# Banded attention with a gated MLP on one core: first values and w_in loaded as whole rows, all loads on SyncE in a planned order

## The chip, the cores and the metric

One core of a Trainium2 chip runs the whole kernel in one launch. The metric is the device time of one execution in microseconds, taken as the median of several runs. Next to it there is one execution recorded by the hardware profiler, from which all rows below come.

## The reference

For 8 batches of 576 positions and 8 heads of 64 columns, attention looks back over a band (32 positions in the first four heads; 128 positions, every fourth one, in the other four). Its output goes through a gated MLP whose gate mixes positions:

```python
scores = where(mask, q @ k.T / sqrt(64), -1e9);  attn = softmax(scores);  x = attn @ v      # x: 8 x 576 x 512
h = maximum(x @ w_in, 0)                          # w_in 512 x 1024
u, v = h[..., :512], h[..., 512:]
v_n = (v - mean(v)) / sqrt(var(v) + 1e-6)
v_s = einsum('ts,bsd->btd', w_spatial, v_n) + b_spatial[None, :, None]      # w_spatial 576 x 576
out = (u * v_s) @ w_out                           # w_out 512 x 512
```

`w_in` and `w_out` come as 64-bit floats, so each is converted on the chip.

## The kernel before, in words

Every large matrix product is made three times, from a rounded ("high") and a remainder ("low") copy of both factors (`PASSES`), so each weight has to be turned into a high and a low tile first. The tiles are `wi` (w_in), `wo` (w_out) and `wt`, `wa`, `wb` (w_spatial), each ending in h or l.

The work of a batch is cut into strands, Python generators that ask for one engine at a time:
- `unit`: scores, maximum, exponential, sum, scaling and transposition of a third of a group of two head pairs. There are six in a batch (group 0 and group 1, three thirds each). PE does the scores at L558, the maximum's subtraction at L623 and the transposition at L573.
- `weighted` (L708): the product with the values of one group, 152 small matmuls. `evacuated` takes the result from PSUM into `xt`.
- `v_tile` (L772): the second half of `x @ w_in`, in five tiles of positions; `gate` (L839, L849 to L851): the first half, and the mixing of positions; `project` (L874): the product with `w_out`, and the store of `ob` to `out`.
- `weight` turns one 128 x 512 part of `w_in` or `w_out` (64-bit) into high and low: ACT L420, L450 and L455, DVE L424 and L426, and two more operations (an add at L433 or L436, a subtraction at L369 or L372) that go to POOL where the table `BY_POOL` has an 'a' or an 's' and else to DVE. `spatial` does the like with `w_spatial`, with the table `EXTRA` for the engine.
- `heads_in`, `values_in`, `weight_in` and `spatial_in` load keys and queries (`kq`), values (`val`), 64-bit weights and `w_spatial` (`stage`).

The class `Timeline` (a planner that runs when the program is built) decides the order on every engine: it always takes the strand with the least value of predicted start plus 0.196 times its rank. `SHIFTS` moves single ranks, `LOADS` sets the order of the first loads. What the planner fixes is the order alone; on the chip each instruction waits on semaphores.

Three things about the loads matter here. `values_in` makes four DMAs for each pair of heads, each of 32 rows with 9 strips of 256 bytes (72 KB), into one of three `val` buffers. `weight_in` needs one of four `stage` buffers, which are idle parts of the later `gated` tiles; a half of `w_in` is two DMAs of 64 rows by 4 KB, one issued by SyncE (L385) and one by ScalarE's queue (L396). A buffer is given back when its conversion is done. The stores of `ob` (L881 to L886) are issued by SyncE where the planner happens to reach them: they take no time of its DMA resource. [...]

`warm` (L896) puts matmuls of zeros on PE at the start, up to a planned time of 20 us, whenever nothing else is ready by the plan.

Of the kernel before, what the change touches and what calls it, by code (L numbers as in the profile page):

```python
# [13 lines left out]
F32 = mybir.dt.float32  # L14
# [46 lines left out]
LOADS = [0, 1, 2, 3, 5, 10, 4, 6, 9, 16, 8, 12, 14, 17, 22, 15, 19, 20, 25, 18, 7, 21, 24, 11, 26, 23, 13]  # L61
BY_POOL = {
    (0, 0): '', (0, 1): 'as', (0, 2): 'a', (0, 3): 'as', (1, 0): '', (1, 1): 'as',
    (1, 2): 'as', (1, 3): 's', (2, 0): 's', (2, 1): 'as', (2, 2): 'a', (2, 3): 'a',
}
EXTRA = {
    ('soft', 0, 0, 0): 0, ('soft', 0, 0, 1): 0, ('soft', 0, 0, 2): 0, ('soft', 0, 1, 0): 0, ('soft', 0, 1, 1): 0, ('soft', 0, 1, 2): 0,
# [944 lines left out]
```

## Time and profile before

| what | value |
|---|---|
| median of 3 runs | 577.76 us (577.19 to 841.0) |
| the profiled execution's own time | 578.02 us |
| its span | 576.2 us |
| PE busy in the span | 547.3 us (95%), 7826 matmuls |
| DVE, ACT, POOL busy | 291.6, 222.1, 130.0 us |

The span runs from the first to the last recorded event; the other 1.82 us of the profiled execution lie around it. PE's busy time is the sum of its matmuls' durations, so 28.9 us of the span have no matmul at all. [...]

### The profile page before, as it was taken

Reading aid. Unit: us, or ns where it says so; the run is one execution under the profiler, and the core shown is the slowest. Engines: PE = TensorE matmul, PEld = TensorE weight load, DVE = VectorE, ACT = ScalarE, POOL = GpSimd, SP = SyncE. Lnnn points to the kernel's source line nnn. Section 1 sums busy time; section 2 is a strip of 40 time slices with the busy share of each in tenths; the row PEclk is TensorE's granted clock in tenths of the full one; section 3 lists DMA queues with packets and bytes.
Section 4 is the critical chain, followed back from the end, with each engine's and each line's share of the span. In section 5 each row is a group of like instructions: output and inputs, shape, how many; then the busy total and the mean of one; then the engine's idle time right before and its main releaser. Section 6 shows DMA issues by size and latency. Waiting matters only on the chain.

```text
span 576.2 us, 17989 instructions
## 1 busy us (share of the span) xinstructions
PE 547.3 (95%) x7826; PEld 500.2 (87%) x7826; DVE 291.6 (51%) x735; ACT 222.1 (39%) x557; POOL 130.0 (23%) x161
## 2 busy tenths in 40 slices
PE   7878989999999999999999999996998999999997
PEld 5656879979998789999989879995897899999997
DVE  5766995456466266344365445591645352314220
ACT  2556855334334334242344432251423152224222
POOL 2536761233033023002133101241302100000000
PEclk9969999999999899999999999998999999999999
DMA  8897714232135310012342530124102101001002
GB/s 223 189 232 191 262 36 122 61 131 97 42 80 177 89 38 1 1 63 76 118 128 51 160 76 1 41 69 126 55 22 53 23 3 52 7 25 42 22 11 83
DMA packets 62882, 47.20 MB, mean 82 GB/s; under 512 B 43730, under 2 KB 52946, under 8 KB 62804
## 3 DMA queue, kind: packets, MB, share of 16 engines
q1 hardware_dynamic: 62164, 43.97, 27.3%
q10 hardware_dynamic: 640, 2.10, 1.4%
q8 instruction: 61, 1.00, 0.7%
q14 instruction: 17, 0.14, 0.1%
HBM read 36.61 MB, written 9.44 MB: 80 GB/s over the span
## 4 chain that ended last, share of the span: by engine, by line
PE 81%; DMA 8%; DVE 6%; issue 2%; SPq 2%; ACT 1%; ACTq 0%; DVEq 0%
PE bank L874 17%; PE bank L849 17%; PE bank L839 17%; PE bank L772 14%; PE bank L708 5%; PE bank L558 5%; DMA stage<-in_w_in_dram 3%; PE bank L573 3%; DMA val<-in_vw_dram 2%; PE bank L851 1%; PE bank L850 1%; DMA kq<-in_qT_dram 1%; SPq L546 1%; DVE mid L426 1%; PE bank L623 1%
## 5 line engine op out<-in xcount | busy, mean ns | idle before, releaser
L874 PE MATMUL bank<-gh,woh 128*128 128x288 f32 x256 | 78.6, 307 | 0.1
L854 DVE TENSOR_TENSOR ur<-ur,bank 128x288 f32<-128x288 f32 x64 | 28.9, 451 | 98.0 <-PE bank L851 98.0
L839 PE MATMUL bank<-xth,wih 128*128 128x288 f32 x256 | 77.8, 304 | 0.4 <-DVE vs L369 0.4
L849 PE MATMUL bank<-wth,vnh 128*128 128x288 f32 x256 | 77.0, 301 | 0.0
L874 PE MATMUL bank<-gl,woh 128*128 128x288 f32 x256 | 76.0, 297 | 0.1
L874 PE MATMUL bank<-gh,wol 128*128 128x288 f32 x256 | 76.0, 297 | 0.0
L849 PE MATMUL bank<-wth,vnl 128*128 128x288 f32 x256 | 75.5, 295 | 0.0
L849 PE MATMUL bank<-wtl,vnh 128*128 128x288 f32 x256 | 75.4, 295 | 0.0
L839 PE MATMUL bank<-xth,wil 128*128 128x288 f32 x256 | 75.4, 294 | 0.0
L839 PE MATMUL bank<-xtl,wih 128*128 128x288 f32 x256 | 75.4, 294 | 0.0
L790 POOL TENSOR_TENSOR stats<-stats,halfneg 128x1 f32<-128x1 f32 (+1 forms) x37 | 23.3, 631 | 183.7 <-DVE stats L788 183.6
L772 PE MATMUL bank<-wih,xth 128*128 128x512 f32 (+1 forms) x148 | 61.2, 414 | 0.2 <-DVE vnl L369 0.2
L643 POOL TENSOR_TENSOR pg<-pg,nm 128x384 f32<-128x384 f32 x36 | 32.3, 898 | 120.8 <-DVE nm L641 111.5
L772 PE MATMUL bank<-wil,xth 128*128 128x512 f32 (+1 forms) x148 | 59.0, 399 | 0.0
L772 PE MATMUL bank<-wih,xtl 128*128 128x512 f32 (+1 forms) x148 | 58.8, 397 | 0.0
L652 POOL TENSOR_TENSOR pg<-pg,rv 128x384 f32<-128x384 f32 x48 | 42.2, 880 | 73.1 <-DVE rv L650 57.7
L878 ACT COPY ob<-bank 128x288 f32<-128x288 f32 x64 | 25.7, 401 | 75.7 <-PE bank L874 53.2
L860 ACT CAST gh<-ur 128x288 fp32r<-128x288 f32 x64 | 27.3, 437 | 63.5 <-DVE ur L854 54.1
L874 PEld LDWEIGHTS bank<-gh,woh 128*128 128x128 f32 x256 | 48.7, 190 | 1.8 <-ACT gh L860 0.4
L839 PEld LDWEIGHTS bank<-xth,wih 128*128 128x128 f32 x256 | 48.0, 188 | 1.7 <-DVE vs L369 0.5
L874 PEld LDWEIGHTS bank<-gl,woh 128*128 128x128 f32 x256 | 48.8, 191 | 0.6 <-DVE gl L369 0.3
L849 PEld LDWEIGHTS bank<-wth,vnh 128*128 128x128 f32 x256 | 48.2, 188 | 0.7
(105 smaller groups left out, 1099.5 us busy)
## 6 DMA issues: line engine op xcount, KB each, us to landing
val<-in_vw_dram SPq DMA_DIRECT2D x128, 72.0 KB, 2.8
kq<-in_kT_dram SPq DMA_DIRECT2D x30, 304.0 KB, 3.7
kq<-in_qT_dram SPq DMA_DIRECT2D x30, 288.0 KB, 4.0
out_dram<-ob SPq DMA_DIRECT2D x48, 144.0 KB, 1.8
stage<-in_w_in_dram ACTq DMA_DIRECT2D x8, 256.0 KB, 6.1
stage<-in_w_in_dram SPq DMA_DIRECT2D x8, 256.0 KB, 5.5
stage<-in_w_out_dram SPq DMA_DIRECT2D x4, 512.0 KB, 4.5
out_dram<-ob SPq DMA_DIRECT2D x16, 112.0 KB, 1.8
```

Of the source, the lines that this page charges most:

```text
L558: nc.tensor.matmul(s[j][q * QB : q * QB + QB], kq[r, WIN + S :].rearrange("p (u n i t) -> p u t n i", n=2, i=QB, t=US)[:, u, g // 2 % US, ...
L643: nc.gpsimd.tensor_add(flat, flat, nm.unsqueeze(2).broadcast_to([P, 2 * US, KW]))
L652: nc.gpsimd.tensor_mul(flat, flat, rv.unsqueeze(2).broadcast_to([P, 2 * US, KW]))
L708: nc.tensor.matmul(acc[h, j][1][1][i * D : i * D + D, at : at + len(blocks) * QB], values[b, hp][1][r, kb // 2 * D : kb // 2 * D + D], x, ...
L772: nc.tensor.matmul(pm, xt[a][:, c, at : at + m], wi[w][:, c, NF:], start=c == 0 and n == 0, stop=c == NC - 1 and n == 2)
L790: nc.gpsimd.tensor_tensor(rs[:m], rs[:m], halfneg[:m], op=ALU.pow)
L839: nc.tensor.matmul(pu, wi[w][:, c, fs], xt[a][:, c, xs], start=n == 0, stop=n == 3 * NC - 1)
L849: nc.tensor.matmul(pv, vn[c][a][:, fs], wts[w][:, c, ws], start=n == 0, stop=False)
L854: nc.vector.tensor_mul(ur, ur, pv)
L860: nc.scalar.copy(gated[0][:, f, ts], ur)
L874: nc.tensor.matmul(po, wo[w][:, f, ds], gated[a][:, f, ts], start=n == 0, stop=n == 3 * NC - 1)
L878: nc.scalar.copy(ob[1], po)
```

## The change

- The values of batch 0 are loaded as whole rows of 4,608 bytes that hold both halves (j = 0 and 1), 32 rows to a DMA, four DMAs for each pair. They land in the memory of the later `wt` tiles (`wide`), not in `val` buffers. The matmuls read the half that they need.
- `w_in` is loaded in four chunks of 128 whole rows (8 KB a row, both halves of `w_in` at once; two DMAs of 64 rows each). Each chunk has its own place: the two `gated` tiles and the two tiles of the later `wo`. No load of `w_in` waits for a buffer. The `stage` buffers of `w_spatial` and `w_out` come into being when the first two chunks have been converted.
- The conversion of `w_spatial` waits until both `weighted` of batch 0 are done, and that of `w_out` until chunks 2 and 3 are converted, since they write into that memory.
- ScalarE issues no DMA any more. SyncE issues all.
- The planner has a new model of the DMAs, and the stores of `ob` now take a place in SyncE's plan.
- A small activation at the head of ScalarE's program, before the first real one.
- New numbers in `SHIFTS`, `LOADS`, `BY_POOL` (21 instead of 15 of 24 operations on POOL), `EXTRA` (all five low parts of `w_spatial` on POOL, before four) and in some planner costs. With the new order `warm` issues 35 matmuls instead of 6.

```diff
-LOADS = [0, 1, 2, 3, 5, 10, 4, 6, 9, 16, 8, 12, 14, 17, 22, 15, 19, 20, 25, 18, 7, 21, 24, 11, 26, 23, 13]
+LOADS = [0, 1, 17, 4, 2, 21, 18, 14, 3, 16, 8, 15, 5, 13, 20, 6, 9, 19, 22, 7, 11, 12, 10]
 BY_POOL = {
-    (0, 0): '', (0, 1): 'as', (0, 2): 'a', (0, 3): 'as', (1, 0): '', (1, 1): 'as',
-    (1, 2): 'as', (1, 3): 's', (2, 0): 's', (2, 1): 'as', (2, 2): 'a', (2, 3): 'a',
+    (0, 0): 'as', (0, 1): 'as', (0, 2): 'a', (0, 3): 'as', (1, 0): 'a', (1, 1): 'as',
+    (1, 2): 'as', (1, 3): 'as', (2, 0): 'as', (2, 1): 's', (2, 2): 'as', (2, 3): 'as',
 }
...
-        self.free = {"DMA": 1.68, "PE": 1.0}
+        self.free, self.moved = {"DMA": 0.72, "PE": 1.0}, 0.0
...
-        late = 1.15 if engine == "DMA" else 0.0
+        late = 0.1 if engine == "DMA" else 0.0
...
             if s.engine == "DMA":
-                self.queue.append((start, start + cost))
+                first, cost = max(start + 0.9, self.moved), s.request[2]
+                self.moved = max(first + s.request[1], start + cost + 0.7)
+                self.queue.append((first, self.moved))
+                landed = self.moved + 0.9
...
-            stage=[t[:, n * BIG : (n + 1) * BIG] for t in stage for n in range(2)],
+            stage=[],
...
+    stage += [const.tile([P, NC * DM], F32, name=f"wos{n}", tag=f"wo{n}") for n in "hl"]
+    wide = [const.tile([P, 4 * (TAIL + S)], F32, name=f"wide{n}", tag=f"wt{n}") for n in "hl"]
...
-    def weight_in(key, src):
+    def pieces_in(c):
 
+        yield DMA, 3.0, 1.2
+        tile = stage[c]
...
+        for n in range(2):
+            row = (c // 2 * 4 + c % 2 + 2 * n) * D
+            nc.sync.dma_start(
+                place[n * D : n * D + D].bitcast(dtype), w_in[row : row + D].rearrange("r h k -> r (h k)")
+            )
...
+            c = key[2]
+            tl.tally(("read", c), 2, [("chunk", c)], [("stage", stage[c][:, n * BIG : n * BIG + BIG]) for n in range(2)] if c < 2 else [])
...
-        yield [("in", sc)]
+        yield [("in", "sp", sc)] + [("weighted", 0, G) for G in range(NG)] * (sc < 4)
...
     def values_in(b, hp):
 
+        if b == 0:
+            yield DMA, 1.45, 0.6
+            dst = wide[hp // 2][:, hp % 2 * BIG : hp % 2 * BIG + BIG]
+            for n in range(2):
+                k = WIN + (1 - n) * QB
+                for j in range(2):
+                    nc.sync.dma_start(dst[j * D + n * QB : j * D + n * QB + QB], vw[b, hp, k : k + QB])
...
-                                values[b, hp][1][r, kb // 2 * D : kb // 2 * D + D],
+                                values[b, hp][j][r, kb // 2],
...
         nc.scalar.copy(ob[1], po)
         tl.give(*held)
+        yield DMA, 0.42, 0.85 if b % 2 and h == 0 else 0.4
...
+    nc.scalar.activation(turnstile, halfneg, AF.Exp)
     tl.add(0.5, warm())
```

Three places show what the planner made of it. The first is SyncE's own order where the first loads stand. `kq` are keys and queries, `stage` and `wos` are places of `w_in`, `val` and `wide` are values. Before:

```order
L530 DMA kq_78<-in_kT_dram 128x608
L531 DMA kq_78<-in_qT_dram 128x576
L385 DMA stage_65<-in_w_in_dram 64x512 x2
L546 DMA val_79<-in_vw_dram 32x9x64 x4
L546 DMA val_80<-in_vw_dram 32x9x64 x4
L546 DMA val_81<-in_vw_dram 32x9x64 x4
L385 DMA stage_64<-in_w_in_dram 64x512 x2
L530 DMA kq_75<-in_kT_dram 128x608
L531 DMA kq_75<-in_qT_dram 128x576
L385 DMA stage_65<-in_w_in_dram 64x512
L546 DMA val_80<-in_vw_dram 32x9x64 x4
```

The same stretch of SyncE now:

```order
L561 DMA kq_78<-in_kT_dram 128x608
L562 DMA kq_78<-in_qT_dram 128x576
L397 DMA wosl<-in_w_in_dram 64x1024 x2
L576 DMA wideh<-in_vw_dram 32x1152 x4
L397 DMA stage_65<-in_w_in_dram 64x1024 x2
L576 DMA wideh<-in_vw_dram 32x1152 x4
L576 DMA widel<-in_vw_dram 32x1152 x4
L397 DMA wosh<-in_w_in_dram 64x1024 x2
L576 DMA widel<-in_vw_dram 32x1152 x4
L561 DMA kq_75<-in_kT_dram 128x608
```

The fourth pair's values stood behind loads of `w_in` that needed a freed buffer and behind keys of batch 1; they now stand directly behind the last chunk of `w_in`, and nothing ahead of them needs a freed buffer.

The second place is POOL, from its first operation on loaded data. `pg` are the probabilities, `mid` and `wil` belong to the conversion of `w_in`. Before:

```order
L652 TENSOR_TENSOR pg<-pg,rv_0_0_229 128x384
L433 TENSOR_TENSOR mid_84<-mid_85,stage_64 128x512
L652 TENSOR_TENSOR pg<-pg,rv_0_1_269 128x384
L372 TENSOR_TENSOR wil<-mid_84,wih 128x512
L652 TENSOR_TENSOR pg<-pg,rv_0_2_309 128x384
L652 TENSOR_TENSOR pg<-pg,rv_1_0_360 128x384
L433 TENSOR_TENSOR mid_86<-mid_87,stage_65 128x512
L652 TENSOR_TENSOR pg<-pg,rv_1_1_403 128x384
L372 TENSOR_TENSOR wil<-mid_86,wih 128x512
L433 TENSOR_TENSOR mid_82<-mid_83,stage_65 128x512
L652 TENSOR_TENSOR pg<-pg,rv_1_2_452 128x384
```

POOL now, from its first operation on loaded data up to the sixth unit's probabilities, its first two rows left out:

```order
L694 TENSOR_TENSOR pg<-pg,rv_0_0_241 128x384
L462 TENSOR_TENSOR mid_84<-mid_85,stage_64 128x512
L694 TENSOR_TENSOR pg<-pg,rv_0_2_303 128x384
L694 TENSOR_TENSOR pg<-pg,rv_0_1_336 128x384
L462 TENSOR_TENSOR mid_86<-mid_87,wosl 128x512
L382 TENSOR_TENSOR wil<-mid_86,wih 128x512
L694 TENSOR_TENSOR pg<-pg,rv_1_2_395 128x384
L462 TENSOR_TENSOR mid_82<-mid_83,wosl 128x512
L694 TENSOR_TENSOR pg<-pg,rv_1_0_447 128x384
L462 TENSOR_TENSOR mid_84<-mid_85,stage_65 128x512
L694 TENSOR_TENSOR pg<-pg,rv_1_1_495 128x384
```

The two rows left out are a conversion's add and subtraction: seven of them now stand ahead of the sixth unit's probabilities, where there were five.

The third place is SyncE where the last keys and queries of all are loaded, beside the stores of batch 4 (`ob`). Before:

```order
L881 DMA out_dram<-ob_94 128x288
L530 DMA kq_75<-in_kT_dram 128x608
L531 DMA kq_75<-in_qT_dram 128x576
L881 DMA out_dram<-ob_95 128x288
L881 DMA out_dram<-ob_94 128x288
L530 DMA kq_77<-in_kT_dram 128x608
L531 DMA kq_77<-in_qT_dram 128x576
L881 DMA out_dram<-ob_95 128x288
```

The same loads now:

```order
L561 DMA kq_77<-in_kT_dram 128x608
L562 DMA kq_77<-in_qT_dram 128x576
L561 DMA kq_78<-in_kT_dram 128x608
L562 DMA kq_78<-in_qT_dram 128x576
L927 DMA out_dram<-ob_95 128x64
L928 DMA out_dram<-ob_95 128x224
L587 DMA val_80<-in_vw_dram 32x9x64 x4
L925 DMA out_dram<-ob_94 128x288
```

The last keys stood between the stores of batch 4; they now stand ahead of all eight.

## Rows read from the trace of the kernel before

**Rows 1.** Windows: stretch, busy us (instructions) of PE, PEld, DVE, ACT, POOL, clock, DMA.
```profile
0.00:43.30 43.30, 32.25 (x665) 24.76 (x665) 27.77 (x75) 20.19 (x44) 16.79 (x28) 0.88 0.91 215
43.30:100.00 56.70, 52.94 (x787) 46.27 (x783) 43.96 (x95) 38.13 (x104) 30.86 (x30) 1.00 0.53 152
100.00:200.00 100.00, 97.94 (x1801) 88.24 (x1800) 52.43 (x147) 37.75 (x103) 24.06 (x29) 0.99 0.33 97
...
300.00:400.00 100.00, 93.59 (x1450) 85.42 (x1450) 52.36 (x136) 36.57 (x91) 21.90 (x27) 0.99 0.27 79
400.00:572.00 172.00, 170.49 (x1954) 161.94 (x1936) 63.77 (x157) 54.08 (x136) 15.67 (x22) 0.98 0.11 32
```

**Rows 2.** Windows with a lower granted clock, same columns.
```profile
30.00:40.00 10.00, 7.67 (x38) 6.16 (x38) 5.93 (x12) 5.63 (x14) 4.49 (x7) 0.50 1.00 220
...
399.50:405.00 5.50, 5.45 (x104) 4.86 (x104) 1.18 (x3) 1.24 (x3) 0.83 (x1) 0.50 0.00 0
```

**Rows 3.** Chain of waits: start, us, what; three loads of the start.
```profile
2.59 4.85 DMA stage<-in_w_in_dram
...
32.35 5.56 DMA val<-in_vw_dram
42.30 7.28 DMA stage<-in_w_in_dram
```

**Rows 4.** Timeline of ACT at the start: start, us, what, idle before and releaser.
```profile
7.52 1.28 ACT L420 ACT_TABLE_LOAD   x1 [7.52 <-DMA stage<-in_w_in_dram]
```

**Rows 5.** Timeline of SP at the start (issue times).
```profile
15.17 10.92 SPq L546 DMA_DIRECT2D val<-in_vw_dram  x12
```

**Rows 6.** Timeline of PE at the start.
```profile
1.04 2.93 PE L896 MATMUL bank<-vnl 128*128 128x512 f32 x6 [1.04 <-DVE vnl L313]
...
30.42 0.47 PE L708 MATMUL bank<-pT,val 32*64 32x64 f32 x17 [2.68 <-issue]
...
40.60 1.05 PE L708 MATMUL bank<-pT,val 32*64 32x64 f32 x72
42.27 1.09 PE L708 MATMUL bank<-pT,val 32*64 32x64 f32 x80 [0.61 <-ACT turnstile L721]
...
43.63 0.40 PE L772 MATMUL bank<-wil,xth 128*128 128x512 f32 x1
43.87 0.39 PE L772 MATMUL bank<-wih,xtl 128*128 128x512 f32 x1
```

**Rows 7.** Windows for the DMA rate (last two columns: share of 16 engines, GB/s).
```profile
15.00:26.00 11.00, 9.21 (x227) 7.31 (x228) 7.75 (x20) 7.52 (x18) 4.99 (x5) 1.00 0.87 169
2.00:16.00 14.00, 10.54 (x166) 7.10 (x164) 8.45 (x33) 4.37 (x8) 1.91 (x6) 1.00 1.01 261
...
91.00:92.00 1.00, 1.00 (x10) 1.00 (x9) 0.03 (x1) 1.00 (x8) 0.00 (x0) 1.00 0.97 289
```

**Rows 8.** Timeline of SP and of PE at the last keys.
```profile
387.14 4.73 SPq L881 DMA_DIRECT2D out_dram<-ob  x3
...
395.06 0.38 SPq L530 DMA_DIRECT2D kq<-in_kT_dram  x1
399.55 0.75 PE L558 MATMUL bank<-kq 64*32 64x64 f32 x34 [4.84 <-DMA kq<-in_qT_dram]
```

**Rows 9.** Windows: the first 5 us, and up to the weights' conversion; columns as in rows 1.
```profile
0.00:5.00 5.00, 3.38 (x12) 2.12 (x15) 2.51 (x13) 0.00 (x0) 2.21 (x13) 1.00 0.60 163
...
0.00:86.00 86.00, 71.19 (x1257) 57.48 (x1257) 64.32 (x148) 50.48 (x111) 44.80 (x55) 0.94 0.75 189
43.30:86.00 42.70, 38.94 (x598) 32.72 (x593) 36.56 (x73) 30.28 (x68) 28.01 (x27) 1.00 0.58 164
```

**Rows 10.** Groups of POOL, 0 to 86 us: busy us, mean ns, idle before and releasers.
```profile
L433 POOL TENSOR_TENSOR mid<-mid,stage 128x512 uint32<-128x512 uint32 x8 | 10.6, 1327 | 6.7 <-DVE mid L426 3.5 <-DMA kq<-in_qT_dram 1.3 <-ACT stage L450 1.1
L652 POOL TENSOR_TENSOR pg<-pg,rv 128x384 f32<-128x384 f32 x10 | 9.4, 944 | 19.8 <-DVE rv L650 15.9 <-DMA kq<-in_qT_dram 1.9 <-ACT gh L860 1.6
```

**Rows 11.** One line of DVE: ns of one min/median/max, first and last start.
```profile
L426 DVE SCALAR_TENSOR_TENSOR mid<-mid,mid x12: 651/693/1686, 10.0 to 78.4; 128x512 uint32<-128x512 uint32 x12
```

More of the change, by code (lines that the diff above doesn't have):

```diff
@@ L208, in run @@
                         o.worth = None
+            landed = None
             if s.engine == "DMA":
-                self.queue.append((start, start + cost))
+                first, cost = max(start + 0.9, self.moved), s.request[2]
+                self.moved = max(first + s.request[1], start + cost + 0.7)
+                self.queue.append((first, self.moved))
+                landed = self.moved + 0.9
             self.free[s.engine] = s.issued = start + cost
-            self.now = s.ready = start + cost + (sum(s.request[2:]) if s.engine == "DMA" else 0.0)
+            self.now = s.ready = landed or start + cost
             got = [(t, heapq.heappop(self.stock[t])[2]) for t in s.tags]
@@ L354, in tile_banded_attention_gated_moe, with settled @@
     wi = [const.tile([P, NC, DFF], F32R, name=f"wi{n}") for n in "hl"]
-    wo = [const.tile([P, NC, DM], F32R, name=f"wo{n}") for n in "hl"]
-    wts = [const.tile([P, 4, TAIL + S], F32R, name=f"wt{n}") for n in "hl"]
+    wo, wts = [], []
+    stage += [const.tile([P, NC * DM], F32, name=f"wos{n}", tag=f"wo{n}") for n in "hl"]
+    wide = [const.tile([P, 4 * (TAIL + S)], F32, name=f"wide{n}", tag=f"wt{n}") for n in "hl"]
+    def settled(tiles, name, shape):
+        if not tiles:
+            tiles.extend(const.tile(shape, F32R, name=f"{name}{n}", tag=f"{name}{n}") for n in "hl")
     was = const.tile([P, TAIL + S], F32R, name="wa")
     wbs = const.tile([P, TAIL + S], F32R, name="wb")
-    wt, wa, wb = [w[:, :, TAIL:] for w in wts], was[:, TAIL:], wbs[:, TAIL:]
+    wa, wb = was[:, TAIL:], wbs[:, TAIL:]
     vb = const.tile([P, NF], F32R, name="vb")
@@ L376, in tile_banded_attention_gated_moe @@
     staged = {}
-    def weight_in(key, src):
-        yield "stage"
-        (staged[key],) = yield DMA, 2.1 if len(src) == 1 else 1.4, 1.5
-        dtype = src[0].dtype
-        place = staged[key][1][:, : 512 if dtype == F32 else 1024]
-        rows = P // len(src)
-        nc.sync.dma_start(place[:rows].bitcast(dtype), src[0])
-        if len(src) > 1:
-            landed = tl.now
-            tl.now -= 1.5 + 1.4
-            tl.add(0.0, second_half(place[rows:].bitcast(dtype), src[1], ("in", *key)))
-            tl.now = landed
-        else:
-            tl.done("in", *key)
@@ L394, in second_half @@
-    def second_half(place, src, key):
-        yield ACT, 0.07
-        nc.scalar.dma_start(place, src)
-        tl.now += 2.9
-        tl.done(*key)
-    def weight(key, hi, lo, dtype, pool):
-        yield [("in", *key)]
+    def pieces_in(c):
+        yield DMA, 3.0, 1.2
+        tile = stage[c]
+        dtype = w_in.dtype
+        words = 1 if dtype == F32 else 2
+        place = tile[:, : 2 * NF * words]
+        for n in range(2):
[3 more added lines that the diff above has]
+            )
+        for half in range(2):
+            staged["wi", half, c] = place[:, half * NF * words : half * NF * words + NF * words]
+        tl.done("in", c)
@@ new lines, in weight_in, with read @@
+    def weight_in(c):
+        yield "stage"
+        (big,) = yield DMA, 1.3, 0.35
+        place = big[1][:, : 512 if w_out.dtype == F32 else 1024]
+        nc.sync.dma_start(place.bitcast(w_out.dtype), w_out[c * P : c * P + P, 0])
+        staged["wo", c] = place
+        slots["wo", c] = [big]
+        tl.done("in", "wo", c)
+    slots = {}
+    def read(key):
+        if key[0] == "wo":
+            tl.give(*slots[key])
+        else:
+            c = key[2]
+            tl.tally(("read", c), 2, [("chunk", c)], [("stage", stage[c][:, n * BIG : n * BIG + BIG]) for n in range(2)] if c < 2 else [])
@@ L410, in weight @@
             sub(lo, w, hi)
-            tl.give(big, *mid)
+            read(key)
+            tl.give(*mid)
             tl.done(*key)
             return
-        words = big[1][:, :1024].rearrange("p (c w) -> p w c", w=2)
+        words = w.rearrange("p (c w) -> p w c", w=2)
         slot, f, g = mid
@@ L436, in weight @@
             nc.vector.tensor_add(f, g, low)
-        tl.give(big)
+        read(key)
         yield [("hi", *key)]
@@ L479, in spatial @@
         if sc < 4:
+            settled(wts, "wt", [P, 4, TAIL + S])
+            wt = [x[:, :, TAIL:] for x in wts]
             nc.scalar.copy(wt[0][:, sc, :], w)
@@ L537, in values_in @@
     def values_in(b, hp):
+        if b == 0:
[5 more added lines that the diff above has]
+                    nc.sync.dma_start(dst[j * D + n * QB : j * D + n * QB + QB], vw[b, hp, k : k + QB])
+            values[b, hp] = [dst.rearrange("p (t j d) -> p t j d", j=2, d=D)[:, :, j] for j in range(2)]
+            tl.done("values", b, hp)
+            return
         yield "val"
-        (big,) = yield DMA, 1.6, 1.5
+        (big,) = yield DMA, 1.33, 3.0
         src = vw[b, hp].rearrange("k (t j d) -> k t j d", j=2, d=D)
@@ L630, in unit @@
                 )
-            yield ACT, 0.72
+            yield ACT, 0.68
             for j in range(2):
@@ L634, in unit @@
             tl.give(*held)
-            yield DVE, 0.9
+            yield DVE, 1.05
         else:
@@ L721, in weighted @@
                 nc.scalar.copy(turnstile, runs_end)
-        tl.give(probs[b, G], *(values[b, hp] for hp in pairs))
+        tl.give(probs[b, G], *(x for hp in pairs for x in slots.get(("val", b, hp), ())))
+        tl.done("weighted", b, G)
         for h in range(2):
@@ L902, in tile_banded_attention_gated_moe @@
     AO, AS = 0.1, 0.6
+    nc.scalar.activation(turnstile, halfneg, AF.Exp)
     tl.add(0.5, warm())
     first = [heads_in(0, hp, lo, hi) for lo, hi in ((0, 1), (1, NU)) for hp in (0, 1)]
-    halves = {}
+    first += [pieces_in(0), heads_in(0, 2), values_in(0, 0), values_in(0, 1), heads_in(0, 3), pieces_in(1)]
+    first += [values_in(0, 2), values_in(0, 3), pieces_in(2), pieces_in(3)]
+    first += [spatial_in(c) for c in range(5)] + [weight_in(c) for c in range(NC)]
     for half in (1, 0):
-        cols = slice(half * NF, half * NF + NF)
         for c in range(NC):
-            heads = [c // 2 * 4 + c % 2 + n for n in (0, 2)]
-            src = tuple(w_in[h * D : h * D + D, half] for h in heads)
-            halves[half, c] = weight_in(("wi", half, c), src)
             r = -1.05 if half else R1[0]
-            tl.add(r + c * R1[1], weight(("wi", half, c), wi[0][:, c, cols], wi[1][:, c, cols], w_in.dtype, BY_POOL[half, c]))
-    first += [heads_in(0, 2), halves[1, 0], heads_in(0, 3), values_in(0, 0), values_in(0, 1), halves[1, 1]]
-    first += [halves[1, 2], values_in(0, 2), halves[1, 3], values_in(0, 3)] + [halves[0, c] for c in range(NC)]
-    first += [spatial_in(c) for c in (0, 1, 2, 3, 4)]
-    first += [weight_in(("wo", c), (w_out[c * P : c * P + P, 0],)) for c in range(NC)]
+            tl.add(r + c * R1[1], weight(("wi", half, c), w_in.dtype, BY_POOL[half, c]))
     for n, at in enumerate(LOADS):
@@ L922, in tile_banded_attention_gated_moe @@
     for c in range(NC):
-        tl.add(R1[3], weight(("wo", c), wo[0][:, c, :], wo[1][:, c, :], w_out.dtype, BY_POOL.get((2, c), "as")))
+        tl.add(R1[3], weight(("wo", c), w_out.dtype, BY_POOL.get((2, c), "as")))
     for c in range(5):
```

28 lines of the change are left out of this document (17 added, 11 removed), and 60 rows, old and new, of the table SHIFTS.

## The prediction

> **What bounds the kernel now.** I read the windows first. PE is busy for 52.94 of 56.70 us in 43.3 to 100, 97.94 of 100 in the next stretch and 170.49 of 172 near the end, but only 32.25 of 43.30 us at the start [rows 1]. So the kernel is bound by PE, and what an order or a load can give back is PE's idle time and its slow time: 11.1 us idle up to 43.3, 3.8 up to 100, and 2.1, 6.4 and 1.5 us in three later stretches. [...]
>
> The chain of waits tells what holds the start: loads. A half of w_in stands in it for 4.85 us from 2.59, strips of values for 5.56 us from 32.35 (so landed at 37.91), another half for 7.28 us from 42.30 [rows 3]. ScalarE's own DMA holds it too: its table load comes at 7.52, after a load of w_in [rows 4]. SyncE needs 10.92 us to issue twelve DMAs of value strips [rows 5], 0.91 us for 72 KB, and in that stretch the DMA engines move 169 GB/s, against 261 in the stretch before it [rows 7]. PE then does the second group's product with the values from 40.60 to 43.36 [rows 6]. I take that point as the end of the start: behind it the positions' tiles follow without a load in their way.
>
> **The change part by part.** *The load stream (-10 us).* Ahead of and with the last values SyncE now issues: keys and queries of batch 0, 2 x (112 + 96) + 2 x (192 + 192) + 2 x (304 + 288) = 2368 KB; w_in, 4 x 512 = 2048 KB; values, 16 x 144 = 2304 KB. That is 6720 KB, 6.88 MB. None of it waits for a buffer. At the 261 GB/s of the row for 2 to 16 us it takes 26.4 us, from 2 us on: landed at 28.4. Values cost more bytes than before (twice), but a DMA carries 144 instead of 72 KB. Add 0.5 us for the wait and 2.8 us for the product (40.60 to 43.36), with three tile matmuls between its halves at 0.24 us [rows 6], 0.7: the point comes at 32.4 instead of 43.36, 11.0 us earlier. Nine tile matmuls are done by then, where there were twelve: 0.7 back. Gain 10.3; I take 10. Bounds: at 289 GB/s (row 91 to 92) the stream ends at 25.8 and the gain is 12.9; at the 169 of the value stretch [rows 7] it ends at 42.7, and the kernel loses 4.
>
> *What must keep up.* The six units need their exponentials; ACT no longer stands behind its own DMAs [rows 4], so I add nothing. The wait of 2.68 us inside a group's product [rows 6] may come back: I take it as hidden, since the first group's product now stands at about 24 us, ahead of the last values; not hidden it takes 2.7 of the 10.
>
> *Conversions to POOL (0, if POOL fills up).* Six operations of w_in and w_out and one of w_spatial go from DVE to POOL, 7 x 1.33 = 9.3 us more on POOL [rows 10]. POOL did 44.8 us of work up to 86 [rows 9], now 54.1. Up to the point at 32.4 its order holds 11 conversion steps (14.6 us), six scalings of probabilities (6 x 0.94 = 5.7) and 2.2 us of masks in the first 5 us [rows 9], 22.5 in all. So 31.6 us are left for the stretch to 76 (86 less 10), which is 43.6 us: a share of 0.72. Before it was 28.01 of 42.70, 0.66 [rows 9]. I count this as covered, at no cost, because DVE sheds the same seven operations; uncovered it is the first rival.
>
> *Fill matmuls (0).* 29 more matmuls of zeros. Six took 2.93 us [rows 6], 0.49 each, so 14 us if all stood in the way; in the idle 11.1 us of the start they cost nothing. They can be a gain as well: a PE that is not idle kept clock 1.00 in the stretch 43.3 to 100 [rows 1]. I take 0, with bounds of +3 and -4 (the 30 to 40 window at full clock would need 3.8 us less, half of its 7.67).
>
> *The stores in SyncE's plan (-4 us).* At 387.14 three stores of `ob` occupy SyncE for 4.73 us, and keys behind them go out at 395.06; PE waits 4.84 us for them and then runs 5.5 us at clock 0.50, which costs another 2.7 [rows 2, 8]. That is 7.6 us for one order. The last keys now stand ahead of all stores of that batch. But every rank is new, and what is late next can't be read from an order: the other idle time in 100 to 572 is of the same kind. I take half of the 7.6, with bounds of -10 (nearly all idle time there goes) and +4 (as much again appears).
>
> *The rest (0).* Converting w_spatial only after the values' use costs nothing while PE has the tiles and gates to do; it is in POOL's share above. The early activation moves 1.28 us of ACT [rows 4] into its idle time.
>
> Sum: 576.2 - 10 - 4 = 562.2 of span, and with the 1.82 us around it 564.0. The profiled execution (578.02) is 0.26 over the median, so against the median 563.8; I say 564.
>
> On the engines that issue, the rows show ScalarE held until 7.52 by its own load [rows 4]. [...]
>
> **The rivals.**
> *POOL becomes the bound of the start.* If POOL is no denser than before (0.66), its 31.6 us take 48.2, and the last weight is ready at 80.6 instead of 76: head gain 5.4, say 5; with the stores' 4 that is 569. For it: POOL's idle time is mostly waiting for DVE and ACT [rows 10]. Against: loads that land earlier take such waits away.
>
> *POOL and DVE slow each other (slower than before).* One place: conversions between 32 and 86. The DVE step at L426 takes 693 ns in the median and up to 1686 [rows 11], though its shape is always the same. If more POOL work makes more such steps, POOL waits for DVE in turn. The point from which it decides: at a share of 31.6 / 53.6 = 0.59 the head gains nothing, and each hundredth below that costs about a microsecond. At 0.50 the last weight is ready at 95.6, 9.6 us later than before, and even with 4 us from the stores the time is 584. Against it: DVE itself has seven operations less.
> [...]
>
> *The loads don't come earlier.* The change would then not do what it says: twice the bytes of values at the 169 GB/s of the value stretch [rows 7] put the last values at 42.7, the point at 47, and the head loses 4, which the stores give back: 578. Milder, at 215 GB/s (the middle of the two rows), the stream ends at 34.0 and the head gains 4.7: 569. For it: 261 is from a stretch with rows of 1 to 4 KB only in part. Against: that stretch already holds short rows, and long ones ran at 289. I use 573.
>
> *Everything late goes away too.* Head -10, later stretches -10 (10.0 us idle in three stretches, and the slow clock with it): 558. For it: a plan that knows of the stores. Against: other orders have other waits.
>
> **How the numbers follow.** Forecast 0.51 (its own range 557 to 571); POOL as the bound 0.19; loads not earlier 0.11; everything late gone 0.13; POOL and DVE 0.06. Two per cent of the median is 11.6 us, about what a measurement of this kernel tells from no change: faster means under 566.2, slower over 589.3. Under 566.2 lie some 0.37 of the forecast's 0.51, all of the 0.13 and 0.05 of POOL as the bound: 0.55. Over 589.3 lies half of the last: 0.03. The rest, 0.42, is within 2%. The range: 553 (below the fourth rival by 5 us, for a head gain of 12.9) to 576 (most of the third rival); left out are 0.05 below and 0.12 above.
>
> **What would show it.** Right: the second group's product ends at 31 to 34; the first 30 us move about 260 GB/s; no window of 5 us at clock 0.50 before 60; no wait of several microseconds for keys behind 300. Wrong: values landing after 35 us; POOL over 90% busy with PE idle between 40 and 80; DVE's step at the line of L426 with a median near its old maximum; new waits of PE for keys or values after 100 us that add up to 6 us or more.

## The result and the profile after

The kernel after takes 572.16 us (569.7 to 572.52), the kernel before 577.76: a ratio of 0.9893, with a 95% interval of 0.9857 to 0.993. So 5.6 us were gained where 13.8 were forecast: the time lies inside the range of 553 to 576, but the gain is less than half of the forecast, and it is within the 2% that the prediction counted as no change. (The 841.0 us in the table of before is one slow execution; the comparison leaves it out.) The profiled execution took 570.54 us, its span is 568.8 instead of 576.2. In the new program the product with the values stands at L750 (L708 before), scores at L600 (L558), the transposition at L615, the tiles of positions at L815, `project` at L917.

Windows of the kernel after; the first two meet where the second group's product with the values ends (43.3 in [rows 1], 46.4 here):

```profile
0.00:46.40 46.40, 35.85 (x690) 28.83 (x690) 26.39 (x70) 19.92 (x45) 20.73 (x29) 0.78 0.99 247
46.40:100.00 53.60, 51.80 (x821) 44.95 (x815) 46.85 (x96) 37.56 (x101) 36.01 (x37) 1.00 0.49 142
100.00:200.00 100.00, 98.61 (x1645) 89.34 (x1644) 49.43 (x133) 37.15 (x97) 23.79 (x29) 1.00 0.31 92
300.00:400.00 100.00, 97.45 (x1721) 88.38 (x1723) 56.98 (x151) 38.94 (x99) 25.32 (x32) 1.00 0.25 71
...
100.00:565.00 465.00, 459.67 (x6351) 427.02 (x6350) 217.23 (x564) 164.58 (x411) 83.87 (x104) 1.00 0.21 62
```

The start did not shrink, it grew by 3.1 us, and with nine tile matmuls done instead of twelve. PE's idle time in it hardly changed (10.6 us, before 11.1); the granted clock, a share of full speed, did: 0.78 instead of 0.88, so (1 - 0.78) x 35.85 = 7.9 us of slow clock against 3.9. (In a second profile of the kernel after, its first 46.4 us have 12.4 us of idle time and a clock of 0.85, so how the loss is shared between the two changes from execution to execution.) Behind 100 us PE is idle for 5.3 us of 465, and the clock is 1.00. The kernel before had 2.1, 6.4 and 1.5 us of idle time in three of the stretches there [rows 1] and a slow clock in two places. So the gain is late.

PE's timeline of the kernel after around the two products:

```profile
29.54 0.46 PE L600 MATMUL bank<-kq 64*32 64x64 f32 x13 [2.66 <-issue]
...
38.53 1.00 PE L750 MATMUL bank<-pT,wideh 32*64 32x64 f32 x46 [3.10 <-issue]
...
43.35 1.22 PE L750 MATMUL bank<-pT,widel 32*64 32x64 f32 x72
...
45.39 1.09 PE L750 MATMUL bank<-pT,widel 32*64 32x64 f32 x80
46.41 0.50 PE L815 MATMUL bank<-wih,xth 128*128 128x512 f32 x1
```

The wait without a releaser (the profile calls it issue) that stood once before [rows 6] now stands twice, 5.8 us together. Which loads were in flight, by the list of DMA issues from 0 to 45 us (KB each, median us to landing):

```profile
stage<-in_w_in_dram SPq DMA_DIRECT2D x4, 512.0 KB, 9.9
...
wosl<-in_w_in_dram SPq DMA_DIRECT2D x2, 512.0 KB, 9.1
wosh<-in_w_in_dram SPq DMA_DIRECT2D x2, 512.0 KB, 7.1
```

`w_in` is eight DMAs of 512 KB, 4096 KB, and not four. The windows with the rate:

```profile
10.00:16.00 6.00, 3.35 (x106) 2.26 (x104) 3.61 (x6) 3.35 (x7) 2.35 (x2) 0.92 1.09 341
16.00:34.00 18.00, 14.50 (x258) 12.14 (x258) 12.25 (x31) 8.37 (x20) 9.50 (x10) 0.69 1.01 234
30.00:40.00 10.00, 6.64 (x163) 5.77 (x164) 6.04 (x12) 3.43 (x10) 5.46 (x5) 0.50 1.00 243
40.00:44.00 4.00, 4.00 (x75) 3.36 (x77) 2.63 (x6) 3.79 (x9) 0.49 (x1) 0.70 1.04 392
```

SyncE's issue of the last values:

```profile
31.07 1.97 SPq L576 DMA_DIRECT2D widel<-in_vw_dram  x4
```

In 16 to 34, when `w_in` and values are on the way and the next keys go out only at 33.17, 234 GB/s pass at a full share of the DMA engines. The last values go out at 31.07 to 33.04 and land some 7 us later, about 40. From there to 44 it is mostly keys, `w_spatial` and `w_out`, each DMA 128 rows and 288 to 512 KB, and 392 GB/s pass.

What PE waited for behind 100 us in the kernel before (us in total, times, longest):

```profile
PE bank L558 <- DMA kq<-in_qT_dram: 5.4, 2, 4.8
PE bank L708 <- DMA val<-in_vw_dram: 2.7, 6, 0.9
PE bank L708 <- issue: 1.7, 2, 1.1
PE bank L558 <- issue: 0.6, 1, 0.6
```

The same view of the kernel after:

```profile
PE bank L750 <- issue: 2.0, 2, 1.3
PE bank L917 <- issue: 1.9, 2, 1.1
PE bank L600 <- DMA kq<-in_qT_dram: 0.8, 2, 0.5
PE bank L600 <- issue: 0.6, 1, 0.6
```

Waits for loads fell from 8.1 to 0.8 us; waits without a releaser rose from 2.3 to 4.5. With two windows of the kernel before at a lower clock this closes the account:

```profile
195.00:205.00 10.00, 9.69 (x171) 8.22 (x172) 3.79 (x10) 2.52 (x7) 1.09 (x2) 0.83 0.30 75
395.00:410.00 15.00, 10.45 (x231) 9.46 (x236) 5.71 (x15) 2.57 (x7) 3.32 (x4) 0.77 0.27 88
```

(1 - 0.83) x 10 and (1 - 0.77) x 15 are some 5 us as a bound of what the clock cost (the second window is partly idle; by 5 us slices it is 4.3 in all). Idle time behind 100 fell by 5.2 (10.5 to 5.3). Together about 9.5 us gained late; the span fell by 7.4; so the first 100 us lost about 2. The rows of the start say the same: 3.1 us later, three tile matmuls fewer (0.7), and 2.0 us less idle time from there to 100 (1.8 instead of 3.8).

### The profile page after: what moved, and what is told of

It reads as the page before. It is cut to its first block, busy times and chain, and to the rows that moved or that the text cites. A ratio compares the mean times of both kernels' runs of the same rounds, so it can differ in the third digit from the quotient of the medians.

```text
span 568.8 us, 18036 instructions
## 1 busy us (share of the span) xinstructions
PE 547.9 (96%) x7855; PEld 501.2 (88%) x7855; DVE 290.5 (51%) x728; ACT 222.5 (39%) x558; POOL 140.6 (25%) x168
## 4 chain that ended last, share of the span: by engine, by line
PE 85%; DVE 4%; DMA 4%; issue 3%; ACT 1%; SPq 1%; POOL 1%; POOLq 0%; ACTq 0%; DVEq 0%
PE bank L917 18%; PE bank L815 17%; PE bank L892 16%; PE bank L882 16%; PE bank L750 6%; PE bank L600 5%; PE bank L615 3%; DMA kq<-in_qT_dram 2%; DMA stage<-in_w_in_dram 1%; PE bank L894 1%; PE bank L893 1%; DVE mid L455 1%; PE bank L665 1%; DVE mid L453 1%; DMA stage<-in_w_spT_dram 1%
## 5 line engine op out<-in xcount | busy, mean ns | idle before, releaser
L917 PE MATMUL bank<-gh,woh 128*128 128x288 f32 x256 | 77.8, 304 | 1.1 <-issue 1.1
L917 PE MATMUL bank<-gl,woh 128*128 128x288 f32 x256 | 75.5, 295 | 0.8 <-issue 0.8
L917 PE MATMUL bank<-gh,wol 128*128 128x288 f32 x256 | 75.4, 294 | 0.0
L833 POOL TENSOR_TENSOR stats<-stats,halfneg 128x1 f32<-128x1 f32 (+1 forms) x37 | 25.0, 675 | 156.7 <-DVE stats L831 156.3
L815 PE MATMUL bank<-wih,xth 128*128 128x512 f32 (+1 forms) x148 | 61.2, 413 | 0.0
L815 PE MATMUL bank<-wil,xth 128*128 128x512 f32 (+1 forms) x148 | 58.1, 393 | 0.0
L815 PE MATMUL bank<-wih,xtl 128*128 128x512 f32 (+1 forms) x148 | 58.0, 392 | 0.0
L379 DVE TENSOR_TENSOR gl<-ur,gh 128x288 fp32r<-128x288 f32 x64 | 30.3, 481 | 40.9 <-ACT gh L903 40.8
L917 PEld LDWEIGHTS bank<-gh,woh 128*128 128x128 f32 x256 | 48.1, 188 | 2.8 <-issue 1.4
L917 PEld LDWEIGHTS bank<-gl,woh 128*128 128x128 f32 x256 | 48.1, 188 | 1.2 <-issue 1.0
L885 ACT ACTIVATE ur<-bank 128x288 f32<-128x288 f32 x64 | 26.3, 411 | 58.0 <-PE bank L882 57.4
```

Of the source, the lines that this page charges most:

```text
L379: nc.vector.tensor_sub(out, a, b.bitcast(F32))
L815: nc.tensor.matmul(pm, xt[a][:, c, at : at + m], wi[w][:, c, NF:], start=c == 0 and n == 0, stop=c == NC - 1 and n == 2)
L885: nc.scalar.activation(ur, pu, AF.Relu)
L917: nc.tensor.matmul(po, wo[w][:, f, ds], gated[a][:, f, ts], start=n == 0, stop=n == 3 * NC - 1)
```

## The experiments

**Three for the start: shape, bytes, fills.** First `w_in` in one DMA of 128 rows per chunk, the rows put in that order by the host:

```diff
-        for n in range(2):
-            nc.sync.dma_start(place[n * D : n * D + D]..., w_in[row : row + D]...)
+        nc.sync.dma_start(place..., w_in[c * P : c * P + P]...)
```

> Each chunk of w_in comes as one DMA to all 128 partitions instead of two DMAs to 64 each (the layouts put the rows of a chunk side by side); bytes, place in SyncE's order and every other engine's order are unchanged. Theory A (bytes: the stream ahead of the last values is 8.98 MB, because w_in is 4.19 MB and not the 2.1 MB of the forecast, and it is bound by bytes at about 235 GB/s whatever the shape): the rate from 16 to 34 us stays near 235 GB/s and the time stays within 1 us of the changed kernel's 572. Theory B (shape: loads to half of the partitions run at about 230 GB/s, loads to all at about 400, as the rows for 16 to 34 us and for 12 to 14 us of the changed kernel have it): w_in's 4.19 MB take 10.5 instead of 18.2 us, so the last values land up to 8 us earlier, and the time falls by 4 to 8 us. [...]

565.74 us, ratio 0.9792 (0.974 to 0.9844). Its windows:

```profile
10.00:16.00 6.00, 5.33 (x120) 4.23 (x119) 5.33 (x11) 3.13 (x9) 4.87 (x4) 1.00 1.05 388
16.00:34.00 18.00, 12.74 (x334) 10.44 (x333) 13.66 (x32) 9.56 (x25) 10.78 (x10) 0.83 1.00 312
```

PE at the end of its second product (L746 here):

```profile
38.75 1.09 PE L746 MATMUL bank<-pT,widel 32*64 32x64 f32 x80
```

The same bytes, the same issuer and order: 312 instead of 234 GB/s, the product ends at 39.84 instead of 46.48, and the time is 6.4 us below the kernel after's, inside B's 4 to 8. B holds, and A, one rate for all shapes, falls. The DMAs are now also half as many and twice as large; but keys and `w_out`, in DMAs no larger than the 512 KB of the halves, passed at 392 GB/s above, so size alone does not make the difference.

Next half of `w_in`'s bytes. The kernel leaves out the load of the first half and converts the second half's data in its place, so `u` is not the right one:

```diff
-                place[n * D : n * D + D]..., w_in[row : row + D]...
+                place[n * D : n * D + D, NF * words : 2 * NF * words]..., w_in[row : row + D, 1]
```

> Only the second half of w_in is loaded (64 rows by 4 KB in each DMA); the first half's conversion works on the second half's data, so what u is computed from is left out. The order on every engine is unchanged. The stream ahead of the last values is then 6.88 MB, the size that the forecast worked with. Theories A and B alike: it ends 2.1 MB / 0.23 = 9 us earlier, the second group's product with the values ends 6 to 10 us earlier than 46.4, and the time falls by 6 to 10 us. Theory C: PE's two waits of 2.66 and 3.10 us without a releaser stay and the time falls by less than 2 us.

563.29 us, 0.9744 (0.9693 to 0.9796), 8.9 us below the kernel after, as A and B had it. The second product ends at 38.07; of the waits without a releaser in the first 50 us 0.5 us is left, so C, by which these waits and not the loads hold the start and would stay, falls. PE waits 3.5 us for scaled probabilities from POOL instead. With the bytes that the prediction had counted, the point comes at 38, not at 32.4: the loads were not the only thing in the way.

Then six fill matmuls instead of 35:

```diff
-            nc.tensor.matmul(... z ...)
+            made += 1
+            if made <= 6:
+                nc.tensor.matmul(... z ...)
```

> Only the first 6 of the 35 fill matmuls of zeros are issued; all else is in the same order. If they cost nothing and give nothing, the time stays within 1 us of the changed kernel's. If they stand in the way of the first units (PE is busy with them from 7.9 to 11.0 us), it falls by 1 to 3 us. If they keep the clock up where it counts, it rises by 1 to 4 us. [...]

567.67 us, 0.981 (0.975 to 0.987): 4.5 us below the kernel after, a larger fall than any of the cases foresaw, though the two intervals just overlap. In the start nothing is better, the second product ends at 46.48. The gain is late: in 100 to 400 PE is idle for 1.5 us, where the kernel after has 5.3. Why fills at the start matter behind 100 us is taken up below.

**Values in strips of 256 bytes again**, in the same place:

```diff
-                    nc.sync.dma_start(dst[j * D + n * QB : ...], vw[b, hp, k : k + QB])
+                    nc.sync.dma_start(dst.rearrange("p (t j d) -> p t j d", ...)[...], vw[b, hp].rearrange(...)[k : k + QB, :, j])
```

> The values of batch 0 come as strips of 256 bytes again (half the bytes), from the same place in SyncE's order into the same memory. Theory A (bytes): 1.18 MB less at 235 GB/s, so the last values land 5 us earlier and the time falls by 2 to 4 us. If whole rows are what helps, as the forecast had it: at the 169 GB/s that strips ran at before, 1.18 MB take 7.0 us instead of 2.36 MB at 235 taking 10.0, so the strips would still be 3 us faster in the stream, unless SyncE's issue (0.91 us for each of 16) holds them: then 14.6 us, 4.6 us later, and the time rises by 2 to 5 us.

570.11 us, 0.9857 (0.9807 to 0.9907): 2.05 us below the kernel after, at the lower edge of A's 2 to 4 and not clear of noise. 195 GB/s in 16 to 34; half the bytes at a lower rate, and the product ends at 44.15. Whole rows did not help against strips here; if anything they cost a little.

**The stores alone, in the kernel before:** ScalarE issues the eight stores of batch 4.

```diff
-            nc.sync.dma_start(out[b, ds, ts], ob[1])
+            (nc.scalar if b == 4 else nc.sync).dma_start(out[b, ds, ts], ob[1])
```

> The kernel before, with the eight output stores of batch 4 issued by ScalarE, so that SyncE is not held by them and issues the keys' loads of the last batches without that stop. Theory S (the stores on SyncE hold back the keys and the values' loads, and the clock falls in the wait): TensorE's 4.84 us wait for keys at 394.7 and the clock of .50 behind it go, and the time falls from 577.8 by 4 to 8 us, to 570-574, which is nearly the whole difference between before and after. Rival K (something else, the memory in which the keys lie, keeps these loads late): the wait stays within 1 us of 4.84, time 577-579. Rival P (TensorE's own waits without a releaser move and eat the gain): the wait goes, but waits without a releaser behind 100 us grow from 2.3 us to 4 or more, time 573-577.

574.86 us (572.0 to 577.08), 0.9941 (0.991 to 0.9972): a gain of 2.6, not of 4 to 8. Its windows:

```profile
55.00:65.00 10.00, 9.04 (x82) 6.50 (x83) 9.25 (x25) 8.33 (x18) 9.10 (x10) 0.83 0.51 139
395.00:405.00 10.00, 8.68 (x186) 7.58 (x189) 3.67 (x9) 4.25 (x10) 1.58 (x2) 1.00 0.18 62
340.00:345.00 5.00, 5.00 (x42) 4.96 (x30) 2.83 (x8) 1.83 (x7) 0.00 (x0) 0.66 0.28 63
```

The wait of 4.84 us [rows 8] and the slow clock behind it [rows 2] are gone: theory S is right about this place, where idle time and slow clock together fall from 7.8 us to 1.3 (385 to 410, by slices of 5 us). The median fell by only 2.6. This profile has about 4 us more of idle time and slow clock in 55 to 65 and 340 to 345 than the kernel before, but the first store that the edit moves goes out at 390.96: both stretches lie ahead of it, so they are a difference between two executions and not the price of the change. Rival P's time came, its reason did not: waits without a releaser behind 100 us are 2.8 us, not 4. Why the median gained less than this place is not shown.

**Two issuers for `w_in`:** the second half of each chunk by ScalarE.

```diff
-            nc.sync.dma_start(
+            (nc.scalar if n else nc.sync).dma_start(
```

> The kernel after, with the second 64-row half of each of the four w_in chunks issued by ScalarE instead of SyncE, so that the two halves of one chunk go side by side in two queues. [...] Rival A (the queue's order doesn't matter, since a queue already works on several transfers at once): 16-34 us stays at 225-245 GB/s, time 570-573. Rival C (the four issues in front of ScalarE's table load and its first conversion hold ScalarE up): its first conversion starts over 2 us later than the 11.59 of after, time 572-576.

576.04 us (574.03 to 577.38), 0.9965 (0.9939 to 0.9991): some 4 us above the kernel after. Two windows:

```profile
5.00:15.00 10.00, 1.26 (x18) 0.46 (x18) 1.63 (x10) 0.00 (x0) 0.00 (x0) 0.70 1.04 220
15.00:20.00 5.00, 5.00 (x52) 4.23 (x53) 1.87 (x5) 1.48 (x4) 0.00 (x0) 0.57 1.01 333
```

ScalarE issued its four halves within its first 3 us, so they went ahead of everything else, at 220 GB/s, and keys came late: the first conversion starts at 16.97. The run tells little of two halves side by side; C was right in its size, for another reason (the order of the transfers).

**The planned place of the stores, undone in the kernel after.**

```diff
-        yield DMA, 0.42, 0.85 if b % 2 and h == 0 else 0.4
...
+        tl.now += 2.5
```

> The kernel after, with the plan of before for the output stores: they take no DMA time in it, and its clock is moved on by 2.5 us behind each pair. Only the order on SyncE changes, and with it two names of banks in the late batches. Theory S (the planned place of the stores is what ended the late waits for keys): waits for keys and values behind 100 us grow from 0.8 us to 4 or more and the clock falls below 1.00 in one of the late stretches, time 575-579. Rival T (the issue by SyncE of everything and the loads' due times did that; the stores' place is a detail): these waits stay under 2 us, time 570-574.

575.99 us (572.07 to 579.78), 0.9972 (0.9934 to 1.0009): inside S's times. The waits for keys and values behind 100 us are 2.2 us, between the two theories' bounds of 4 and 2. The same again, beside an unchanged kernel after:

> The kernel after, unchanged, beside the next run on the same chip. If 572.16 holds elsewhere, 570-574 and a ratio to before of .986 to .994; if the kernel after differs from chip to chip by its waits without a releaser, up to 577.

> The kernel after with the stores outside the plan's DMA time, a second time. Theory S (the planned place of the stores is worth time): 3 to 5 us above the kernel after of the same call, with waits for values of 1 us or more behind 100 us. Rival T (the earlier 575.99 was that chip's clock): within 1.5 us of it.

The kernel after: 571.77 us, 0.9917 (0.9881 to 0.9952). Without the plan for the stores: 577.47, 0.9994 (0.9966 to 1.0022). The difference is 5.7 us, as much as the whole change brought: theory S holds, a little above its 3 to 5, with 1.4 us of waits for values. Most of it stands at one place. SyncE in the kernel after, in this profile of it:

```profile
451.94 2.54 SPq L587 DMA_DIRECT2D val<-in_vw_dram  x4
454.58 0.55 SPq L927 DMA_DIRECT2D out_dram<-ob  x1
```

PE behind it:

```profile
458.16 0.91 PE L750 MATMUL bank<-pT,val 32*64 32x32 f32 x60 [0.22 <-DMA val<-in_vw_dram]
```

And the window:

```profile
457.00:470.00 13.00, 12.78 (x203) 10.45 (x203) 4.65 (x12) 3.73 (x10) 1.10 (x2) 1.00 0.12 36
```

SyncE, with the stores where the planner reaches them:

```profile
456.02 0.33 SPq L926 DMA_DIRECT2D out_dram<-ob  x1
456.41 0.51 SPq L927 DMA_DIRECT2D out_dram<-ob  x1
457.01 2.54 SPq L587 DMA_DIRECT2D val<-in_vw_dram  x4
```

PE, with the same load:

```profile
460.87 0.43 PE L750 MATMUL bank<-pT,val 32*64 32x64 f32 x8 [1.08 <-DMA val<-in_vw_dram]
```

And its window:

```profile
457.00:470.00 13.00, 11.50 (x183) 9.04 (x183) 1.30 (x3) 2.73 (x8) 0.00 (x0) 0.74 0.22 57
```

A store that goes out at 456.02 only, though SyncE was through with the stores before it at 453.53, now stands ahead of the four loads. They go out 5.1 us later than in the other run, of which 1.7 us are a lag that PE already has here (its tile matmuls ahead of this product start at 458.56, there at 456.83). PE idles 1.3 us more and then runs at a mean clock of 0.74 instead of 1.00: (1 - 0.74) x 11.5 = 3.0 us more. So 4.3 us stand here, of the 6.4 by which these two profiled executions differ.

**Everything in 128 rows.** The first change and one DMA of 128 rows of 2304 bytes for each pair's values, in all batches:

```diff
-            for n in range(2):
-                k = WIN + (1 - n) * QB
-                for j in range(2):
-                    nc.sync.dma_start(dst[j * D + n * QB : j * D + n * QB + QB], vw[b, hp, k : k + QB])
...
+            dst = dst[:, : NS * D]
+            nc.sync.dma_start(dst, vw[b, hp])
```

> The kernel after, with w_in in one DMA of 128 rows per chunk, as in the first run with that change, and the values of all batches too in one DMA of 128 rows of 2304 B per pair, which the host has laid out in the two keys' halves (for the first batch half the bytes of before, the rest unchanged in bytes). The order on the engines stays. Theory B (transfers over all 128 partitions run at about 400 GB/s, those over a half at about 230): the first 34 us carry over 330 GB/s until the stream is done, the last value of the first batch lands before 30 instead of near 39, the second group's product ends at 34-37, time 558-563. Rival A+ (128 rows were faster in w_in only for its long rows): values stay near 230 GB/s, the product ends at 37-39, time 562-565. Rival P (TensorE's waits without a releaser only move into the later stretches): product before 37, but over 5 us of such waits behind 100 us, time 563-568.

560.99 us (559.28 to 562.48), 0.9693 (0.9646 to 0.9741). Windows:

```profile
10.00:16.00 6.00, 6.00 (x124) 4.79 (x122) 5.33 (x10) 3.06 (x8) 4.86 (x4) 1.00 1.04 421
16.00:34.00 18.00, 13.97 (x336) 11.65 (x334) 13.55 (x32) 10.41 (x27) 10.78 (x10) 0.79 0.97 380
34.00:50.00 16.00, 16.00 (x301) 11.71 (x299) 12.20 (x21) 11.02 (x23) 11.72 (x11) 0.92 0.20 59
```

PE, the end of the first group's product (L740 here) and of the second's:

```profile
30.27 0.99 PE L740 MATMUL bank<-pT,wideh 32*64 32x64 f32 x45 [2.13 <-issue]
...
37.98 1.09 PE L740 MATMUL bank<-pT,widel 32*64 32x64 f32 x80
```

380 to 421 GB/s. The last values go out at 12.37 and land 10.2 us later, at 22.6. Values in rows of 2304 bytes, half as long as the kernel after's, go as fast as the rest, so rival A+ with its long rows falls. The product still ends at 39.07, and PE is busy without a gap from 34 on: B's time came, its point in the start did not, since there PE itself has become the bound, with 3.7 us of waits without a releaser and, by slices of 1 us, 4.9 us of slow clock up to that point.

**Fewer fills on top of it**, 6 and 20 instead of 35:

> The kernel with w_in and values in DMAs of 128 rows, with 6 instead of 35 fill matmuls at the start. Theory I (TensorE's waits without a releaser stand at fixed numbers of its instructions, some 127 matmuls apart, and become long where loads are in flight): with 29 matmuls fewer in front, the waits behind 100 us stand at other work and other times than in the run with all 35 (there at 174.7, 192.9 and 318.4, 2.8 us together), while in the start they stay at matmul numbers near 341 and 469; the sum behind 100 us may fall below 1.5 us as it did with six fills before, time 556-560. Rival J (they belong to the work at that place, scores or products with values): they stay at the same lines of the same batch, 2.5-3.5 us together, time 560-562 less nothing.

> The same with 20 fill matmuls, 15 fewer than in the kernel after. Theory I: a third set of places for the waits without a releaser behind 100 us, the first ones again near matmul numbers 341 and 469; time between 556 and 563, and its difference to the runs with 35 and 6 goes with the sum of these waits and the slow clock behind them. Rival J: the same places and sum as with 35, time 560-562.

557.5 us, 0.9662 (0.9624 to 0.9701), and 557.49, 0.9661 (0.9616 to 0.9706). These are the lowest times of all; 3.5 us below the run with 35 fills, though the intervals of the ratios overlap. Where the long wait cuts the first group's product, with 20 fills (with 35 it is shown above):

```profile
26.37 0.80 PE L740 MATMUL bank<-pT,wideh 32*64 32x64 f32 x50 [0.25 <-ACT turnstile L753]
30.64 0.68 PE L740 MATMUL bank<-pT,wideh 32*64 32x64 f32 x30 [3.47 <-issue]
```

With 6:

```profile
25.55 0.91 PE L740 MATMUL bank<-pT,wideh 32*64 32x64 f32 x64 [0.25 <-ACT turnstile L753]
30.16 0.35 PE L740 MATMUL bank<-pT,wideh 32*64 32x32 f32 x16 [3.70 <-issue]
```

With 35 fills 45 of the second 80 matmuls stand behind the wait, with 20 it is 30, with 6 it is 16: for 15 and 29 matmuls fewer in front the cut moves by 15 and by 29. The wait belongs to a number of matmuls from PE's start, not to the work that stands there; J falls. The number can be counted: 473 to 476 matmuls have begun when this wait ends, in 13 of the 14 profiles of this case (all but the run with half of `w_in`), the kernel before among them, where it is the 2.68 us of [rows 6]. Two of the windows, the kernel before and the kernel after:

```profile
0.00:30.42 30.42, 21.89 (x473) 16.47 (x474) 19.19 (x59) 12.70 (x27) 12.72 (x23) 0.99 0.89 205
0.00:38.53 38.53, 27.99 (x474) 22.27 (x474) 23.24 (x63) 14.45 (x32) 17.49 (x27) 0.78 0.96 235
```

Behind 100 us these waits are 2.8 us with 35 fills, 1.6 and 0.8 with 20 and 6; PE is idle for 4.1, 2.2 and 0.8 us of 100 to 550. The two lower times do not follow these sums, as theory I had it: 20 and 6 fills have the same median. With 6 the second product also ends 1.5 us earlier, at 37.54; with 20 it ends at 39.07 as with 35.

## Why the prediction was wrong, step by step

- *The load stream (-10 us).* This step failed, and in two of its terms. "w_in, 4 x 512 = 2048 KB": it is 4096 KB, since each chunk is two DMAs of 512 KB. At 261 GB/s these 2.1 MB put the point 8.0 us later, from 32.4 to 40.4. And the 261 GB/s of [rows 7] were taken for all transfers, though in that stretch the keys' 128 rows stood beside `w_in`. Transfers to 64 or 32 rows went at 234. The stream of 8.98 MB at 234 from 2 us on ends at 40.4, as it did, which puts the point another 4.0 us later, at 44.4. The last 2 us are PE's: behind the wait of 3.10 us, at a mean clock of 0.60 from 38.53 on, it comes to the second group's product at 43.35 only. [Rows 7] gave a sign of the rate: the value stretch with 169 was put down to short strips, but strips against whole rows changed little (195 against 234), and 128 rows took the rate to 380 to 421. The 289 of the row for 91 to 92 was read as the rate of long rows; what SyncE had sent ahead of it, in the kernel before, are keys, over 128 rows of 2.4 KB:

```profile
88.30 0.55 SPq L530 DMA_DIRECT2D kq<-in_kT_dram  x1
```

- The same step took 2.8 us after the last value for the point. With the values landed at 22.6 the product still ended at 39.07: the six units, the tile matmuls put between, waits of 3.7 us and 4.9 us of slow clock fill PE's time until then. So 39.07 does not show that the point of 32.4 was out of reach: without these waits and at full clock it would come at 30.5, by estimate from these sums and if no other engine then held PE. No run had that.
- *What must keep up.* "I take it as hidden" was wrong as well. Two waits of 2.66 and 3.10 us stood in the start. And [rows 4] showed ScalarE waiting for the data of its first conversion, not for its queue: this conversion started at 8.81 before, and now, with no DMA of its own but with a whole chunk to wait for, starts later:

```profile
11.59 0.66 ACT L449 ACTIVATE mid<-stage 128x512 f32<-128x512 f32 x1 [9.36 <-DMA stage<-in_w_in_dram]
```

- *Conversions to POOL (0).* No cost, as forecast: in 46.4 to 100 POOL is busy for 36.01 of 53.6 us, a share of 0.67, and PE has only 1.8 us of idle time. Neither POOL's bound nor its quarrel with DVE came: the DVE step (L426, now L455) has a median of 730 ns after 693 and a maximum of 1699 after 1686.
- *Fill matmuls (0).* On the kernel after, right in the start: the point stands at 46.48 with 35 and with 6. But by their number they shift where PE waits later. Six instead of 35 brought 4.5 us here and 3.5 with all loads over 128 rows, both on the edge of the noise.
- *The stores in SyncE's plan (-4 us).* Right in its mechanism, and near in size: taking the plan away costs the kernel after 5.7 us, by the runs side by side, and moving batch 4's stores alone gave the kernel before 2.6. The whole late gain was 9.5, near the 10 of the rival "everything late goes away too". New waits did come, as feared (4.5 us without a releaser instead of 2.3), and were less than what went.
- *The rivals.* "The loads don't come earlier", with a chance of 0.11, came true in what it says of the start: its values at 42.7 and its point at 47 against 40 and 46.4. This was in part luck: its 6.88 MB at 169 GB/s take 40.7 us where 8.98 MB at 234 take 38.4, so too few bytes and too low a rate cancel. Its 573 beside the measured 572.16 is luck too: it is the middle of a severe and a mild case with 4 us from the stores, where the start lost about 2 and the later stretches gave 9.5. And it looked for the reason in short rows, where the partitions decided: 312 against 234 GB/s in 16 to 34 with the same bytes of `w_in` in rows of the same length.

That SyncE alone issues the loads did not hold the rate down: with everything in 128 rows it reached 421 GB/s in 10 to 16. Longer rows, which the prediction put at 289 GB/s, were not what brought it: in 16 to 34 the rate was 234 GB/s with transfers to 64 and 32 partitions, 312 with `w_in` alone in 128 rows, and 380 with the values in 128 rows too, though their rows were then half as long. Why transfers to fewer partitions were slower was not shown.

What is not settled: the loss of about 2 us in the first 100 comes from two accounts and was not tried by itself, and how the new planner, apart from the stores, ended the late waits for values (2.7 to 0) was not separated from the new ranks.

## What to carry to other kernels

Before a load stream is timed, add up its bytes from the list of DMA issues, count times size, and take the rate from a stretch with the same number of partitions in each transfer: DMAs over 128 rows moved 1.6 times what DMAs over 64 and 32 did in the same stretch (380 against 234 GB/s), and with half the bytes for the first values this was worth 11.2 us, twice the 5.6 of the whole change. Where a queue holds loads and stores, ask of every store which load stands behind it: here the delay of four loads cost 1.3 us of waiting and 3 us of slow clock. And a change of a few instructions at the head of a program can move time hundreds of microseconds later, so a difference of 3 us is no proof for the place that was edited.

## What the runs showed of the hardware

PE's waits without a releaser in the start come at fixed distances in its program: in all profiles those of 1 us or more end some 219, 347, 474 or 601 matmuls from its start (each within two), 127 or 128 apart. The profile's list of DMA queues of the kernel after has a kind of transfer that is about as far apart:

```profile
q8 instruction: 61, 1.00, 0.7%
```

61 packets for 7855 matmuls, one for 129, 16.4 KB each. In the first 50 us one fell into 26 to 27 and one into 35 to 36: the two long waits begin at 26.9 and 35.4. Three more packets fell into 10 to 20 and 40 to 50, where PE had no such wait. With half of `w_in`, 0.5 us of waiting was left in the start. What PE waits for at these places was not shown.

The clock did not follow a wait's length alone: in the kernel after waits of up to 1.3 us behind 100 us left it at 1.00; in its second profile it was 0.66 in 290 to 295, behind a wait of 1.3.
